# Second MoE of a fused kernel: transfers in multiples of 16 rows, an expert order with 384-place ranks computed rows-first, a last slot in halves, weight loads issued behind the token lists

## The chip, the cores and the metric

One core of a Trainium2 chip runs the whole program. The metric is device time in microseconds (us) of that core, as a median over runs. The engines of a core work side by side, each on its own instruction stream: PE (matmul), DVE (vector), ACT (activations and copies), POOL (GpSimd, which also issues indirect DMAs) and SP (which issues plain DMAs). They wait for each other through semaphores.

## The reference, cut to what matters

Attention with hashed buckets and a first, dense mixture of experts run ahead of the part that changes. What changes is the second mixture: 1536 tokens of width 512, 8 experts of hidden width 1024, each token sent to its two best experts.

```python
def _moe2_ref(x, w_gate, w_noise, noise, w1, w2):
    logits = x @ w_gate
    noise_scale = np.log1p(np.exp(x @ w_noise))
    noisy_logits = logits + noise_scale * noise
    top2 = np.argpartition(-noisy_logits, 2, axis=1)[:, :2]
    ...                                   # softmax over the two: top2_w
    out = np.zeros((N, D), dtype=np.float32)
    for e in range(E):
        for k in range(2):
            mask = top2[:, k] == e
            h = np.maximum(x[mask] @ w1[e], 0.0)
            out[mask] += top2_w[mask, k, None] * (h @ w2[e])
    return out
```

## The kernel before, in words

Every operand of a large matmul is split in two halves of its mantissa (`hh`/`hl` of the hidden values, `w2h`/`w2l` of the weights, `gh`/`gl` of the gathered tokens), and a product is three matmuls: high by high, high by low, low by high.

The router writes, for each token and each of its two experts, a line (token number, weight) into a table in DRAM; an expert's lines lie one behind the other. The experts are then worked off in eight stages, `e` = 0 to 7. Stage 0 is expert 0; half of its 432 places (`EARLY`, 216, two slots of 108) is run ahead, from the tokens that the router knows first, and the other half when all are known. Stages 1 to 7 take the other experts in the order of their token counts: `rank` sorts them, `order` says which expert a stage takes. `CAPS` gives a stage's places, `SLOTS` the number of slots into which they are cut, and `ROWS` the rows of one slot (432 in 4 slots of 108, 384 in 3 of 128, 372 in 3 of 124).

The first layer (`hidden_part`, L238, four parts for a stage) has weights as the stationary side and the tokens as columns: 96 matmuls of as many columns as there are places. The second layer exists in two forms.

- **Turned** (`project_turned`, stages 1 to 6): weights are stationary, 96 matmuls of as many columns as there are places. The result has features on partitions, so it is turned in 32 x 32 blocks (`padded`, `yt`), written to a DRAM scratch `yd` by four stores on SP (`store_turned`, L1271), loaded back with a place on each partition (`ya`, `load_turned`, L1276), scaled on DVE and added to the output by indirect DMAs on POOL (`send`, `scatter`, L1053). The load of stage e is issued on SP when part 0 of stage e+1 is in the queue, and its scaling (`xg<-ya` on DVE) and sends are spread over the second layer of stage e+1; for the last stage they stand at part 2.
- **Rows** (`give`, stages 0 and 7): the hidden values are stationary, and a slot is 24 matmuls of 512 columns whose result has tokens on partitions. It is scaled from PSUM and scattered at once.

The tokens of stage 1 come by one gather a slot (`fetch_rows`, L1226) and 4 transposes on PE for each slot (`turn_rows`, L1030). Those of stages 2 to 7 come in blocks of 32 lines (`fetch_blocks`, L1238: 16 or 12 gathers on POOL, issued two stages ahead) and are turned on DVE (`turn_blocks`). The lists of lines that steer all this (`lts` by rows, `li` and `at` by blocks) are loaded by `list_rows` on SP, each behind a register load of the expert's number.

Weights are fetched on SP into a ring of `stage` tiles (`stage_part`, L173, 512 KB each), split by ACT (high, L180) and DVE (low, L184). The four w2 loads of stage e+1 are issued at the end of stage e: three ahead of the `yd` stores, one behind them.

The change of stage from the first mixture to the second goes so. PE ends the first mixture; `choose` picks experts for the last three tiles of tokens, in two calls with `turn_rows` for the early slots among them. Parts 0 to 2 of the early half of stage 0 follow, with `place` writing the last lines of the table among them. Then w2 of expert 0 is split in two pairs around part 3, the late list `lt` is loaded, two gathers fetch the late slots (L1021), and two early slots run through the second layer in rows. In the second of these, after 18 of its 24 matmuls, stand the transposes of the late slots, which wait for the two gathers. In SP's queue the four w1 loads of stage 1 stand between the first list and the others.

The order of each engine's instructions here is the order of the Python code (`manual_schedule`).

Of the kernel before, what the change touches and what calls it, by code (L numbers as in the profile page):

```python
# [9 lines left out]
F32 = mybir.dt.float32  # L10
F32R = mybir.dt.float32r
BF16 = mybir.dt.bfloat16
I32 = mybir.dt.int32
# [10 lines left out]
CAPS = (432, 432, 416, 400, 400, 384, 384, 372)  # L24
SLOTS = (4, 4, 4, 4, 4, 3, 3, 3)
# [3 lines left out]
ROWS = [c // n for c, n in zip(CAPS, SLOTS)]  # L29
NBLOCK = 4 * SLOT_S  # L30
# [11 lines left out]
def lsh_attention_moe_kernel(ctx, tc, qk, v, proj, probs, w1, w2, w_gate, w_noise, noise, w1b, w2b, out):  # L42
# [45 lines left out]
    caps = const.tile([P, E2], F32, name="caps")  # L88
    for e in range(E2):
        nc.gpsimd.memset(caps[:, e:e + 1], float(CAPS[e]))  # L90
    cum = const.tile([P, E2], F32, name="cum")
# [59 lines left out]
    yd = dram.tile([CAP, DM], F32, name="yd")  # L151
# [112 lines left out]
    def project(o, parts, wt, cols, f0=0, f1=None):  # L264
        for f in range(f0, NF if f1 is None else f1):
            g, ff = divmod(f, 2)
            hh, hl = parts[g]
            wh, wl = wt[g]
            nc.tensor.matmul(o, hh[:, ff, cols], wh[:, ff], start=(f == 0), stop=False)
            nc.tensor.matmul(o, hh[:, ff, cols], wl[:, ff], start=False, stop=False)  # L270
            nc.tensor.matmul(o, hl[:, ff, cols], wh[:, ff], start=False, stop=(f == NF - 1))
# [754 lines left out]
    def turn_rows(rows, s, xgs, n=ROWS[0]):  # L1026
        gh, gl = rows
        pt = small()
        for d in range(ND):
            nc.tensor.transpose(pt[:, d * P:d * P + n], by_chunk(xgs[s], d), ident[:n, :n])  # L1030
# [10 lines left out]

    def put(pool, tag, bufs, ps, lt, s, e):
# [7 lines left out]
    def scatter(y, ps, lt, s, e, view=None):  # L1050
        nc.vector.tensor_scalar_mul(y if view is None else view, ps, lt[:, s, 1:2].bitcast(F32))
        nc.gpsimd.memset(apart, 0.0)
        ins = nc.gpsimd.indirect_dma_start(out=out, out_offset=bass.IndirectOffsetOnAxis(ap=lt[:, s, 0:1], axis=0),  # L1053
# [36 lines left out]
    def rank():  # L1090
# [5 lines left out]
        nc.vector.tensor_tensor(who, key[:, 1:].unsqueeze(1).to_broadcast(sh), iota8[:, 0:K].unsqueeze(2).to_broadcast(sh),  # L1096
# [16 lines left out]
    with tc.manual_schedule(engines={mybir.EngineType.PE}):  # L1113
# [79 lines left out]
    padded = [mp.tile([P, SLOT_S, 4, 32], F32, name=f"padded{i}", bufs=1) for i in range(2)]  # L1193
# [7 lines left out]
    at = mp.tile([P, E2, 4, SLOT_S], I32, name="at", bufs=1)  # L1201
    nc.gpsimd.memset(li, 0)

# [248 lines left out]
```

## Time and profile before

| what | value |
|---|---|
| median of 3 runs | 1089.43 us (1087.86 to 1090.86) |
| profiled execution | 1089.52 us |
| its span, first to last instruction | 1087.8 us |
| mean granted clock of PE | 0.99 |
| PE busy | 1055.6 us, 97% of the span |
| DVE / ACT / POOL busy | 721.2 / 504.9 / 359.0 us |

PE is busy nearly throughout, so what counts are the short stretches in which it stands still or runs at a lower granted clock, the number and width of its matmuls, and what is left to do after its last one. Over the whole span those stretches drown in the means; they are read from the timeline and from windows laid between two first matmuls of neighbouring layers.

### The profile page before, as it was taken

Reading aid. Unit: us, or ns where it says so; the run is one execution under the profiler, and the core shown is the slowest. Engines: PE = TensorE matmul, PEld = TensorE weight load, DVE = VectorE, ACT = ScalarE, POOL = GpSimd, SP = SyncE. Lnnn points to the kernel's source line nnn. Section 1 sums busy time; section 2 is a strip of 40 time slices with the busy share of each in tenths; the row PEclk is TensorE's granted clock in tenths of the full one; section 3 lists DMA queues with packets and bytes.
Section 4 is the critical chain, followed back from the end, with each engine's and each line's share of the span. In section 5 each row is a group of like instructions: output and inputs, shape, how many; then the busy total and the mean of one; then the engine's idle time right before and its main releaser. Section 6 shows DMA issues by size and latency. Waiting matters only on the chain. (4 is left out here: it accounts for less than half of the span.)

```text
span 1087.8 us, 15954 instructions
## 1 busy us (share of the span) xinstructions
PE 1055.6 (97%) x5835; PEld 961.1 (88%) x5836; DVE 721.2 (66%) x1353; ACT 504.9 (46%) x918; POOL 359.0 (33%) x364
## 2 busy tenths in 40 slices
PE   8999999999999999999999999999889999999995
PEld 6999999988888888899888888988778999999993
DVE  7999999978666656647765667545525556765760
ACT  6999999963433333432433342222213334443440
POOL 6587666620000000000000003115336478655533
PEclk9999999999999999999999999999989999999997
DMA  4644444244532112214212225014156468688864
GB/s 134 156 118 117 117 117 118 59 117 135 174 101 78 58 59 78 78 39 136 78 59 59 78 64 164 25 50 79 31 140 183 120 197 219 179 225 222 238 169 56
DMA packets 92781, 125.69 MB, mean 116 GB/s; under 512 B 15882, under 2 KB 59722, under 8 KB 92286
## 3 DMA queue, kind: packets, MB, share of 16 engines
q1 hardware_dynamic: 82522, 110.43, 35.5%
q0 software_dynamic: 9888, 13.92, 6.6%
q8 instruction: 48, 0.79, 0.3%
q14 instruction: 35, 0.29, 0.1%
q10 hardware_dynamic: 288, 0.26, 0.1%
HBM read 92.66 MB, written 20.11 MB: 104 GB/s over the span
## 5 line engine op out<-in xcount | busy, mean ns | idle before, releaser
L182 POOL TENSOR_SCALAR w1h<-stage 128x1024 fp32r<-128x1024 f32 x4 | 5.0, 1257 | 419.4 <-PE sm L723 419.4
L459 DVE TENSOR_TENSOR el<-sm,eh 128x384 fp32r<-128x384 f32 x192 | 102.7, 549 | 17.2 <-ACT eh L458 15.8
L184 DVE TENSOR_TENSOR w2l<-stage,w2h 128x1024 fp32r<-128x1024 f32 x64 | 77.6, 1223 | 49.0 <-ACT w2h L180 35.6
L1238 POOL DMA_INDIRECT xb<-x2d,at x84 | 95.5, 1137 | 25.2 <-issue 24.5
L248 PE MATMUL big<-gh,w1h 128*128 128x216 f32 (+5 forms) x288 | 95.8, 333 | 0.0
L249 PE MATMUL big<-gl,w1h 128*128 128x216 f32 (+5 forms) x288 | 95.1, 330 | 0.0
L250 PE MATMUL big<-gh,w1l 128*128 128x216 f32 (+5 forms) x288 | 95.1, 330 | 0.0
L458 ACT CAST eh<-sm 128x384 fp32r<-128x384 f32 x192 | 86.9, 479 | 16.0 <-PE sm L455 15.4
L728 ACT ACTIVATE hh<-mx 128x384 fp32r<-128x384 f32 x72 | 37.8, 525 | 118.3 <-DVE mx L814 59.6
L403 PE MATMUL big<-k,q 128*128 128x512 f32 (+1 forms) x384 | 90.9, 358 | 1.6 <-POOL k L389 0.7
L455 PE MATMUL sm<-ident,ex 128*128 128x128 f32 x576 | 90.6, 274 | 1.7 <-DVE el L459 1.0
L410 DVE TENSOR_SCALAR_CACHE_REDUCE ms<-big 128x768 f32<-128x768 f32 x96 | 91.0, 948 | 1.8 <-PE big L403 1.5
L422 ACT ACTIVATE ex<-ms,mn 128x768 f32<-128x768 f32 x96 | 90.5, 942 | 3.3 <-DVE ms L410 2.8
L184 DVE TENSOR_TENSOR w1l<-stage,w1h 128x1024 fp32r<-128x1024 f32 x62 | 75.9, 1224 | 19.7 <-ACT w1h L180 16.9
L741 PE MATMUL big<-w2l,hh 128*128 128x512 f32 x224 | 88.4, 395 | 0.0
L742 PE MATMUL big<-w2h,hl 128*128 128x512 f32 x224 | 88.2, 394 | 0.0
L740 PE MATMUL big<-w2h,hh 128*128 128x512 f32 x224 | 88.2, 394 | 0.0
L455 PEld LDWEIGHTS sm<-ident,ex 128*128 128x128 f32 x576 | 70.2, 140 | 12.7 <-DVE el L459 5.6
L253 ACT ACTIVATE hh<-big 128x768 fp32r<-128x768 f32 (+5 forms) x44 | 34.2, 776 | 92.6 <-PE big L250 71.7
L255 DVE SCALAR_TENSOR_TENSOR hl<-big,hh 128x768 fp32r<-128x768 f32 (+5 forms) x44 | 40.1, 910 | 53.9 <-ACT hh L253 49.6
L722 PE MATMUL sm<-xth,w1h 128*128 128x384 f32 x192 | 66.4, 346 | 3.1 <-DVE xa L519 1.2
L1262 PE MATMUL sm<-hl,w2h 128*128 128x400 f32 (+3 forms) x192 | 66.5, 346 | 2.4 <-DVE hl L255 2.4
(289 smaller groups left out, 2929.1 us busy)
## 6 DMA issues: line engine op xcount, KB each, us to landing
stage<-in_moe_w_dram SPq DMA_DIRECT2D x100, 512.0 KB
stage<-in_moe_w_dram SPq DMA_DIRECT2D x58, 256.0 KB
k<-q SPq DMA_DIRECT2D x45, 192.0 KB
z<-in_qk_dram SPq DMA_DIRECT2D x15, 384.0 KB
out_dram<-zero SPq DMA_DIRECT2D x4, 1024.0 KB
vr<-in_v_dram SPq DMA_DIRECT2D x16, 192.0 KB
share<-norms SPq DMA_DIRECT2D x16, 192.0 KB
q<-q SPq DMA_DIRECT2D x15, 192.0 KB
```

Source lines behind the costliest of these rows:

```text
L184: rest.tensor_sub(lo, st, v32(hi))
L248: nc.tensor.matmul(o, wh[:, d, fs], xh[:, d, cols], start=(d == 0), stop=False)
L249: nc.tensor.matmul(o, wh[:, d, fs], xl[:, d, cols], start=False, stop=False)
L250: nc.tensor.matmul(o, wl[:, d, fs], xh[:, d, cols], start=False, stop=(d == ND - 1))
L403: nc.tensor.matmul(ps[:, n0:n1], w_[:, qs], x_[:, n0:n1], start=st, stop=not st)
L410: nc.vector.tensor_scalar(ms, ps[:, :S], MASKED, 3.0e38, op0=ALU.min, op1=ALU.min, accum_out=mn)
L422: nc.scalar.activation(ex, ms, AF.Exp, bias=mn, scale=-1.0, accum_out=recs[u % 2][:, i:i + 1])
L455: nc.tensor.transpose(pt[:, c * P:(c + 1) * P], ex[:, cc * P:(cc + 1) * P], ident)
L459: nc.vector.tensor_sub(el[:, cs, js], ptv, v32(eh)[:, cs, js])
L740: yield lambda: nc.tensor.matmul(outs[j], hh[:, k, js], wh[:, i], start=st, stop=False)
L741: yield lambda: nc.tensor.matmul(outs[j], hh[:, k, js], wl[:, i], start=False, stop=False)
L1238: nc.gpsimd.indirect_dma_start(out=xb[:, b], out_offset=None, in_=x2d.rearrange("t (g x) -> (t g) x", g=4), in_offset=bass.IndirectOffsetO ...
```

## The change

- **Stages and places.** The seven ranks are dealt to the stages by a constant `RANKS`: stage 1 takes the fifth largest expert with 384 places in 3 slots, stages 2 to 5 the four largest (432, 416, 400, 400), stages 6 and 7 the two smallest (384 each, before 384 and 372). Seven more small memsets on POOL in the prologue hold the constant.
- **Second layer by rows.** Where a stage's places are its slots times 128 (`short`: stages 1 and 6, and 7 as before), the second layer runs in rows: `give` for each slot, with no `yd`, `ya` and `send`.
- **Multiples of 16.** In the other stages the loads of `ya` and the sends move `MOVED` rows, which is `ROWS` rounded up to 16 (108, 104 and 100 become 112), and the `yd` stores always move 32 partitions for each block (before 27, 26 or 25). Unused places of `lts` are preset by a memset and an iota on POOL.
- **Last slot in halves.** The last slot of stage 7 runs as two halves of 256 columns, 24 matmuls each; each half is scaled and scattered by itself (rows of 1 KB, `at_half`).
- **Weights behind lists.** The four w1 loads of stage 1 are issued on SP behind all seven lists; the four w2 splits of stage 0 stand ahead of part 3; the second `choose` stands ahead of both `turn_rows`, with 4 filling matmuls (`hum`).

SP, at the change from the first mixture to the second. `lt` is the late list of stage 0, `lts` and `li` the lists of a stage, `stage` the w1 loads of stage 1. Before:

```order
L1016 DMA lt<-table 108x4
L1205 TENSOR_LOAD order
L1205 ISA x2
L1207 ISA
L1207 DMA lts<-table 108x8
L173 ISA
L173 DMA stage<-in_moe_w_dram 128x1024
L173 ISA
L173 DMA stage<-in_moe_w_dram 128x1024
```

and now:

```order
L1021 DMA lt<-table 108x4
L1224 TENSOR_LOAD order
L1224 ISA x2
L1226 ISA
L1226 DMA lts<-table 128x6
L1224 TENSOR_LOAD order
L1224 ISA x2
L1226 ISA
L1226 DMA lts<-table 108x8
L1229 ISA
L1229 DMA li<-table 32x4x8
```

The loads of weights no longer stand behind the first `lts`; the next lists do.

POOL at the same place, where `xg<-x2d,lt` are the late gathers and `xg<-x2d,lts` those of stage 1. Before:

```order
L1195 MEMSET padded_8082 128x512
L1195 MEMSET padded_8083 128x512
L1202 MEMSET li 32x256
L1021 DMA xg<-x2d,lt 108x512 x2
L1226 DMA xg<-x2d,lts 108x512 x4
```

and now:

```order
L1211 MEMSET padded_8092 128x512
L1211 MEMSET padded_8093 128x512
L1219 MEMSET li 32x256
L1220 MEMSET lts 128x64
L1026 DMA xg<-x2d,lt 108x512 x2
L1221 IOTA lts 128x32
L1248 DMA xg<-x2d,lts 128x512 x3
```

A memset of `lts` stands ahead of the late gathers and an iota behind them, which the first `lts` load on SP waits for; stage 1 has three gathers where it had four.

DVE at the end of the program. Before, in stage 7:

```order
L184 TENSOR_TENSOR w2l<-stage,w2h 128x1024
L1051 TENSOR_SCALAR xg<-ya,lts 128x512 x3
L255 SCALAR_TENSOR_TENSOR hl<-big,hh 128x744
L1051 TENSOR_SCALAR xg<-sm,lts 124x512 x3
L1402 TENSOR_LOAD counts
```

and now, in stage 6:

```order
L189 TENSOR_TENSOR w2l<-stage,w2h 128x1024
L1064 TENSOR_SCALAR xg<-ya,lts 112x512 x2
L260 SCALAR_TENSOR_TENSOR hl<-big,hh 128x768
L1064 TENSOR_SCALAR xg<-ya,lts 112x512 x2
L1270 STREAM_TRANSPOSE tb<-xb 128x384
L1274 TENSOR_TENSOR gl<-tb,gh 128x384
```

The scalings of the last turned stage (stage 5) have moved from stage 7 to stage 6; two of them stand ahead of the last `hl` of that stage's first layer.

The diff, cut to its core:

```diff
-CAPS = (432, 432, 416, 400, 400, 384, 384, 372)
-SLOTS = (4, 4, 4, 4, 4, 3, 3, 3)
+CAPS = (432, 384, 432, 416, 400, 400, 384, 384)
+SLOTS = (4, 3, 4, 4, 4, 4, 3, 3)
+RANKS = (4, 0, 1, 2, 3, 5, 6)
 CAP = max(CAPS)
 SLOT_S = max(SLOTS)
 SLOT_P = CAP // SLOT_S
 ROWS = [c // n for c, n in zip(CAPS, SLOTS)]
+MOVED = [-(-r // 16) * 16 for r in ROWS]
...
+    def give_half(y, parts, wt2, lt, s, e, h):
+        ps = small()
+        n = ROWS[e]
+        w = DM // 2
+        hs = slice(h * w, (h + 1) * w)
+        project(ps[:n, :w], parts, wt2, slice(s * n, (s + 1) * n), out=hs)
+        scatter(y[:n, hs], ps[:n, :w], lt[:n], s, e, half=h)
...
-    def scatter(y, ps, lt, s, e, view=None):
+    def scatter(y, ps, lt, s, e, view=None, half=None):
+        rows, o = lt[:, s, 0:1], out
+        if half is not None:
+            rows, o = at_half[:, half:half + 1], out.rearrange("t (h x) -> (t h) x", h=2)
+        ins = nc.gpsimd.indirect_dma_start(out=o, out_offset=bass.IndirectOffsetOnAxis(ap=rows, axis=0),
                                            in_=y, in_offset=None, compute_op=ALU.add)
...
-        nc.vector.tensor_tensor(who, key[:, 1:].unsqueeze(1).to_broadcast(sh), iota8[:, 0:K].unsqueeze(2).to_broadcast(sh),
+        nc.vector.tensor_tensor(who, key[:, 1:].unsqueeze(1).to_broadcast(sh), ranks.unsqueeze(2).to_broadcast(sh),
...
+        chosen.append(choose(tile_logits(turned, 4), t3 + 1, 2))
         first_rows = [ap.tile([P, ND, EARLY], F32R, tag=t, name=t) for t in ("gh", "gl")]
-        turn_rows(first_rows, 0, xgs)
-        chosen.append(choose(tile_logits(turned, 2), t3 + 1, 2))
-        turn_rows(first_rows, 1, xgs)
+        for s in range(early):
+            turn_rows(first_rows, s, xgs)
...
+    at_half = mp.tile([P, 2], I32, name="at_half", bufs=1)
     nc.gpsimd.memset(li, 0)
+    nc.gpsimd.memset(lts, 0)
+    nc.gpsimd.iota(lts[:, :, :, 0], pattern=[[0, E2], [1, SLOT_S]], base=0, channel_multiplier=SLOT_S)
...
-        mine = tv[bass.ds(whose[e], 1), 0:CAPS[e]]
+        mine = tv[bass.ds(whose[e], 1), 0:P * SLOTS[e]]
         nc.sync.dma_start(lts[:ROWS[e], e, :SLOTS[e]].rearrange("p s c -> p (s c)"),
-                          mine.rearrange("o (p s) c -> p (o s c)", s=SLOTS[e]))
+                          mine.rearrange("o (p s) c -> p (o s c)", s=SLOTS[e])[:ROWS[e]])
         if e > 1:
-            nc.sync.dma_start(li[:ROWS[e] // 4, e, :, :SLOTS[e]].rearrange("r b s c -> r b (s c)"),
+            nc.sync.dma_start(li[:, e, :, :SLOTS[e]].rearrange("r b s c -> r b (s c)"),
                               mine.rearrange("o (b r s) c -> r (o b) (s c)", b=4, s=SLOTS[e]))
 
     def list_pieces():
+        for h in range(2):
+            nc.vector.tensor_scalar(at_half[:, h:h + 1], lts[:, E2 - 1, SLOTS[-1] - 1, 0:1], 2.0, float(h),
+                                    op0=ALU.mult, op1=ALU.add)
...
-            xg = slot_tile()[:ROWS[e]]
+            xg = slot_tile()[:MOVED[e]]
             nc.gpsimd.indirect_dma_start(out=xg, out_offset=None, in_=x2d,
-                                         in_offset=bass.IndirectOffsetOnAxis(ap=lts[:ROWS[e], e, s, 0:1], axis=0))
+                                         in_offset=bass.IndirectOffsetOnAxis(ap=lts[:MOVED[e], e, s, 0:1], axis=0))
...
-                            yp[:, :n].rearrange("p s b r -> p (s b) r"))
-
-    def store_turned(yt, e):
+        nc.scalar.copy(yp[:, :, :ROWS[e]], ps[:, :c].rearrange("p (s r) -> p s r", s=n))
+        nc.vector.transpose(yt.rearrange("p s b (k c) -> p k (s b) c", k=ND)[:, d], yp.rearrange("p s (b r) -> p (s b) r", b=4))
+
+    def store_turned(yt):
         for g in range(4):
-            nc.sync.dma_start(yd[0:CAPS[e]].rearrange("(b r s) (g x) -> g r s b x", b=4, s=SLOTS[e], g=4)[g],
-                              yt[32 * g:32 * g + ROWS[e] // 4, :SLOTS[e]])
+            nc.sync.dma_start(yd.rearrange("(b r s) (g x) -> g r s b x", b=4, s=SLOT_S, g=4)[g], yt[32 * g:32 * g + 32])
 
     def load_turned(e):
-        ya = mp.tile([P, SLOT_S, DM], F32, tag="ya", name="ya", bufs=1)[:ROWS[e], :SLOTS[e]]
-        nc.sync.dma_start(ya, yd[0:CAPS[e]].rearrange("(p s) d -> p s d", s=SLOTS[e]))
+        ya = mp.tile([P, SLOT_S, DM], F32, tag="ya", name="ya", bufs=1)
+        nc.sync.dma_start(ya[:MOVED[e]], yd.rearrange("(p s) d -> p s d", s=SLOT_S)[:MOVED[e]])
         return ya
 
 
     def send(s, ya, e):
-        y = slot_tile()[:ROWS[e]]
-        scatter(y, ya[:, s].rearrange("p (g k c) -> p k g c", g=4, k=ND), lts[:ROWS[e], e], s, e,
+        n = MOVED[e]
+        y = slot_tile()[:n]
+        scatter(y, ya[:n, s].rearrange("p (g k c) -> p k g c", g=4, k=ND), lts[:n, e], s, e,
                 y.rearrange("p (k g c) -> p k g c", g=4, k=ND))
+
+    def with_rows(ya, e):
+        return [(s, ya, e) for s in range(SLOTS[e])]
+
+    def short(e):
+        return 0 < e and SLOTS[e] * P == CAPS[e]
 
         wt1 = wt1_next
-        wt2 = [load_w2_part(w2b, 0, r, engine=nc.scalar, staged=staged[r]) for r in (0, 1)]
+        wt2 = [load_w2_part(w2b, 0, r, engine=nc.scalar, staged=staged[r]) for r in range(NP)]
         parts.append(hidden_part(NP - 1, wt1, *first_rows, EARLY, slice(0, EARLY)))
-        wt2 += [load_w2_part(w2b, 0, r, engine=nc.scalar, staged=staged[r]) for r in (2, 3)]
         lt_late, xgs = fetch(mp, SLOT_S, 0, EARLY, early)
         list_rows(1)
-        staged = [stage_part(w1_part(w1b, 1, r), [P, ND, FC]) for r in range(NP)]
         next_xgs = fetch_rows(1)
         for e in range(2, E2):
             list_rows(e)
+        staged = [stage_part(w1_part(w1b, 1, r), [P, ND, FC]) for r in range(NP)]
...
-                if g == 0 and e > 1:
-                    late = [load_turned(e - 1), e - 1]
-                if g == 2 and e == E2 - 1:
-                    for s in range(SLOTS[e - 1]):
-                        send(s, *late)
+                if g == 0:
+                    late = [] if e < 2 or short(e - 1) else with_rows(load_turned(e - 1), e - 1)
+                if g > 1 and short(e):
+                    for _ in range(2 if late else 0):
+                        send(*late.pop(0))
...
+            elif e == E2 - 1:
+                for s in range(SLOTS[e] - 1):
+                    give(mp, "xg", SLOT_S, parts, wt2, lts[:, e], s, e)
+                y = slot_tile()
+                for h in range(2):
+                    give_half(y, parts, wt2, lts[:, e], SLOTS[e] - 1, e, h)
+            elif short(e):
+                prepare(0)
+                for s in range(SLOTS[e]):
+                    prepare(s + 1)
+                    give(mp, "xg", SLOT_S, parts, wt2, lts[:, e], s, e)
+                    fetch_some(s, SLOTS[e])
+                    for r in range(NP * s // SLOTS[e], NP * (s + 1) // SLOTS[e]):
+                        wt1.append(load_w1_part(w1b, e + 1, r, nc.scalar))
             else:
-                for s in range(SLOTS[e]):
-                    give(mp, "xg", SLOT_S, parts, wt2, lts[:, e], s, e)
+                yt = mp.tile([P, SLOT_S, 4, P], F32, tag="yt", name="yt", bufs=1)
+                prepare(0)
+                for d in range(ND):
+                    prepare(d + 1)
+                    project_turned(yt, d, parts, wt2, e)
+                    fetch_some(d, ND)
+                    if late and d > 0:
+                        send(*late.pop(0))
+                    wt1.append(load_w1_part(w1b, e + 1, d, nc.scalar))
+            while late:
+                send(*late.pop(0))
             if 0 < e < E2 - 1:
-                if late:
-                    for s in range(ND - 1, SLOTS[e - 1]):
-                        send(s, *late)
                 ahead = [stage_part(w2_part(w2b, e + 1, r), [P, 2, DM]) for r in range(NP - 1)]
-                store_turned(yt, e)
+                if not short(e):
+                    store_turned(yt)
                 ahead.append(stage_part(w2_part(w2b, e + 1, NP - 1), [P, 2, DM]))
     mp_scope.close()
```

## Rows read from the trace of the kernel before

**Rows 1.** Timeline, PE, at the change to the second mixture (start, us, engine, line, operation, [idle before, releaser])

```profile
763.44 0.73 PE L1030 MATMUL sm<-ident,xg 108*128 108x108 f32 x4 [1.43 <-DMA xg<-x2d,lt]
...
783.73 0.48 PE L269 MATMUL sm<-w2h,hh 128*108 128x512 f32 x1 [0.56 <-ACT w2h L180]
...
784.99 0.49 PE L270 MATMUL sm<-w2l,hh 128*108 128x512 f32 x1 [0.78 <-DVE w2l L184]
...
795.59 0.70 PE L1030 MATMUL sm<-ident,xg 108*128 108x108 f32 x4 [3.70 <-issue]
...
797.83 1.00 PE L1030 MATMUL sm<-ident,xg 108*128 108x108 f32 x4 [1.54 <-DMA xg<-x2d,lt]
...
798.51 0.74 PE L269 MATMUL sm<-w2h,hh 128*108 128x512 f32 x1
```

**Rows 2.** Timeline, POOL: an early gather, and the second of the late ones

```profile
759.66 1.03 POOL L1021 DMA_INDIRECT xg<-x2d,lt  x1 [8.60 <-issue]
...
788.87 1.01 POOL L1021 DMA_INDIRECT xg<-x2d,lt  x1 [0.30 <-issue]
```

**Rows 3.** Timeline, SP's DMA queue: w1 loads of stage 1, the last list

```profile
786.93 2.05 SPq L173 DMA_DIRECT2D stage<-in_moe_w_dram  x4
...
801.53 0.32 SPq L1210 DMA_DIRECT2D li<-table  x1
```

**Rows 4.** Windows, PE (window: us, PE busy (instructions), granted clock, DMA share, GB/s)

```profile
798.51:812.93 14.42, 14.42 (x104) 0.83 0.38 63
844.90:864.33 19.43, 18.99 (x98) 1.00 0.34 108
918.08:935.58 17.50, 17.50 (x98) 1.00 0.77 216
953.14:972.01 18.87, 17.90 (x97) 1.00 0.81 227
988.86:1007.51 18.65, 17.35 (x98) 1.00 0.84 235
1024.31:1041.12 16.81, 16.81 (x98) 1.00 0.81 231
1041.12:1057.49 16.37, 16.37 (x98) 1.00 0.74 193
1057.49:1074.40 16.91, 16.90 (x73) 1.00 0.47 57
```

**Rows 5.** Timeline, DVE and POOL: the last scaling, and two scatters

```profile
1074.43 0.75 DVE L1051 TENSOR_SCALAR xg<-sm,lts 124x512 f32<-124x512 f32 x1 [4.84 <-PE sm L271]
...
1061.21 1.56 POOL L1053 DMA_INDIRECT out_dram<-xg,lts  x1 [0.27 <-issue]
...
1075.49 2.21 POOL L1053 DMA_INDIRECT out_dram<-xg,lts  x1 [3.07 <-DVE xg L1051]
```

**Rows 6.** Windows, POOL, around scatters (window: us, POOL busy, granted clock, DMA share, GB/s)

```profile
1059.50:1066.00 6.50, 3.04 (x4) 1.00 0.99 122
1080.00:1085.00 5.00, 0.00 (x0) 0.50 0.30 47
1085.50:1087.80 2.30, 0.00 (x0) 0.50 0.00 0
```

**Rows 7.** Timeline, ACT and SP's queue: the w2 split, stores and `ya` load, stage 4

```profile
954.61 1.05 ACT L180 CAST w2h<-stage 128x1024 fp32r<-128x1024 f32 x1 [4.83 <-DMA stage<-in_moe_w_dram]
...
939.97 6.35 SPq L1271 DMA_DIRECT2D yd<-yt  x4
...
953.06 0.32 SPq L1276 DMA_DIRECT2D ya<-yd  x1
```

**Rows 8.** Timeline, POOL: a scatter of stage 0, two block gathers

```profile
820.66 1.61 POOL L1053 DMA_INDIRECT out_dram<-y,lt  x1 [16.50 <-DVE y L1051]
...
844.95 0.95 POOL L1238 DMA_INDIRECT xb<-x2d,at  x1 [0.30 <-issue]
...
940.45 1.90 POOL L1238 DMA_INDIRECT xb<-x2d,at  x1 [0.30 <-issue]
```

More of the change, by code (lines that the diff above doesn't have):

```diff
@@ L88, in lsh_attention_moe_kernel @@
     caps = const.tile([P, E2], F32, name="caps")
+    ranks = const.tile([P, E2 - 1], F32, name="ranks")
     for e in range(E2):
         nc.gpsimd.memset(caps[:, e:e + 1], float(CAPS[e]))
+        if e > 0:
+            nc.gpsimd.memset(ranks[:, e - 1:e], float(RANKS[e - 1]))
     cum = const.tile([P, E2], F32, name="cum")
@@ L268, in project @@
             wh, wl = wt[g]
[L269 to L271 removed]
+            nc.tensor.matmul(o, hh[:, ff, cols], wh[:, ff, out], start=(f == 0), stop=False)
+            nc.tensor.matmul(o, hh[:, ff, cols], wl[:, ff, out], start=False, stop=False)
+            nc.tensor.matmul(o, hl[:, ff, cols], wh[:, ff, out], start=False, stop=(f == NF - 1))
     hb = wb = None
@@ L1192, in lsh_attention_moe_kernel @@
     apart = mp.tile([1, 8], F32, name="apart", bufs=1)
-    padded = [mp.tile([P, SLOT_S, 4, 32], F32, name=f"padded{i}", bufs=1) for i in range(2)]
+    padded = [mp.tile([P, SLOT_S, P], F32, name=f"padded{i}", bufs=1) for i in range(2)]
     for t in padded:
@@ L1336, in lsh_attention_moe_kernel, with prepare, fetch_some @@
                 rows = new_rows(CAPS[e + 1])
-            if 0 < e < E2 - 1:
-                yt = mp.tile([P, SLOT_S, 4, P], F32, tag="yt", name="yt", bufs=1)
-                if e + 2 < E2:
-                    xbs[e + 2] = blocks()
-                turn_blocks(rows, 0, e + 1)
-                for d in range(ND):
-                    if d + 1 < ND:
-                        turn_blocks(rows, d + 1, e + 1)
-                    project_turned(yt, d, parts, wt2, e)
-                    if e == 1:
-                        follow(rows[1][:, d])
-                        fetch_blocks(3, 2 * d, 2 * d + 2)
-                    elif e + 2 < E2:
-                        each = SLOTS[e + 2]
-                        fetch_blocks(e + 2, each * d, each * d + each)
-                    if late and 0 < d <= SLOTS[e - 1]:
-                        send(d - 1, *late)
-                    wt1.append(load_w1_part(w1b, e + 1, d, nc.scalar))
-            elif e == 0:
+            if 0 < e < E2 - 1 and e + 2 < E2:
+                xbs[e + 2] = blocks()
+            def prepare(d):
+                if d < ND:
+                    turn_blocks(rows, d, e + 1)
+            def fetch_some(d, n):
+                if e == 1:
+                    follow(rows[1][:, d])
+                    fetch_blocks(3, 8 * d // n, 8 * (d + 1) // n)
+                elif e + 2 < E2:
+                    each = 4 * SLOTS[e + 2]
+                    fetch_blocks(e + 2, each * d // n, each * (d + 1) // n)
+            if e == 0:
                 for s in range(early):
-                    for r in range(s * SLOTS[1] // early, (s + 1) * SLOTS[1] // early):
+                    each = [SLOTS[1] * (s + x) // early for x in (0, 1)]
+                    for r in range(*each):
                         turn_rows(rows, r, next_xgs, ROWS[1])
+                    for r in range(NP * s // early, NP * (s + 1) // early):
                         wt1.append(load_w1_part(w1b, e + 1, r, nc.scalar, staged[r]))
```

18 lines of the change are left out of this document (7 added, 11 removed).

## The prediction

> **What bounds the kernel now.** PE is busy for 97% of the span, so the sum has to come from three things: stretches in which PE stands still or runs at a lower granted clock, the width and number of its matmuls, and what is left after its last one. I read them in this order. First PE's timeline where the first mixture hands over to the second [rows 1]: PE waits 1.43 us for an early gather, 0.56 and 0.78 us for the w2 splits, and then 3.70 and 1.54 us in the middle of a second layer, for the two late gathers. POOL has issued the second of these at 788.87 [rows 2]; PE's transposes of it begin at 797.83, 8.96 us later. For the early gather the same way took 763.44 - 759.66 = 3.78 us. What stands beside the slow one and not beside the fast one are four w1 loads of 512 KB, issued on SP from 786.93 on [rows 3]. Second, windows from one layer's first matmul to the next [rows 4]: the stretch behind the late gathers has a granted clock of 0.83, and two second layers of one width differ (400 columns: 17.50 and 18.87 us; 384 columns: 16.81 and 18.65). Third the tail: PE's last layer ends at 1074.40 [rows 4], the span at 1087.8, 13.4 us later.
>
> **A, the hand-over: -7.1 us.** The second `choose` now stands ahead of the transposes that wait 1.43 us, so its matmuls fill that wait. I take 1.0 of the 1.43 as won, and the chain to the late list and gathers as 1.0 earlier: the second late gather at 787.87 on POOL. The w1 loads leave SP's queue at this point; what stands there now are lists of some KB each, and the loads come behind the last list, at about 801 [rows 3]. If the gather then lands as the early one did, PE has it at 787.87 + 3.78 = 791.65, and after the four transposes (798.51 - 797.83 = 0.68) its matmuls go on at 792.33 instead of 798.51: -6.2. The two w2 waits (1.34 together) lie inside that wait and give nothing more while the gathers end last. Of the clock: 798.51 to 812.93 took 14.42 us at 0.83; at full clock 0.83 x 14.42 = 12.0 to 12.4 would do, so some 2.0 are lost there. PE still pauses for the gathers, only for less long, so I give back 0.5. Stage 1 has three slots instead of four: four transposes fewer, of which a group takes 0.70 [rows 1] and overlaps its neighbours in part: -0.45. Bounds: the gathers were held by something else and only the 1.0 and the 0.45 come, -1.5; all of the gather's excess, the clock and the early wait come, -(6.2 + 0.4 + 2.0 + 0.45 + 1.34) = -10.4. I take the value by the uncontended gather, since it is the same instruction with the same bytes 29 us earlier.
>
> New in POOL's queue there: a memset of `lts` ahead of the late gathers, which falls into the time in which POOL waits for the list, and an iota behind them, for which the first `lts` load on SP waits. Behind that load in SP's queue stand all other lists and the w1 loads. First need of the w1 loads is stage 1's first layer, which PE reaches some 25 us after the late gathers; lists of about 12 us and loads of about 10 us have room there. I cost it at nothing; if not covered, it is the few us by which the lists start later.
>
> **B, PE's work: +0.6 us.** The seven ranks have the same widths in another order, but the last has 384 places instead of 372: its first layer 16.81 instead of 16.37 (16.81 is the same number of matmuls with 384 columns), +0.44 [rows 4]. A second layer by rows is 72 matmuls of 512 columns, 16.91 us, and turned 96 of 384, 16.81: two more stages by rows, +0.2. The halves are 48 matmuls of 256 columns for 24 of 512: at half of 16.91 / 72 = 235 ns they are free, and that I take. The nearest row below 512 is 384 columns at 16.81 / 96 = 175 ns; at that, 48 x (175 - 117) = +2.8. Bounds +0.6 to +3.4.
>
> **C, the stalls in the second layers: -1.65 us.** Stage 1's window holds 19.43 - 18.99 = 0.44 of idle time; stage 4's is 18.87 - 17.50 = 1.37 over its twin, stage 5's 18.65 - 16.81 = 1.84 [rows 4]: 3.65 in all. In stage 4 ACT waits 4.83 us for a w2 tile [rows 7], whose load stands on SP behind the four `yd` stores (6.35 us of issuing). These move 25 partitions each; 32 partitions should spread over more DMA engines, as the 128-row scatters do against the 124-row one [rows 6]. Stage 2 now follows a stage without `yd`, stage 7 too. Against it: more bytes per store, and in stage 6 two scalings of `ya` stand on DVE ahead of the last `hl` of the first layer. `ya` was issued 953.06 - 935.58 = 17.5 us into its stage [rows 4, 7]; with stores that end earlier I estimate 13 (issuing ended 939.97 + 6.35 - 935.58 = 10.7 into the stage, and 2.2 to land as a 128-row scatter does [rows 6]), and the last `hl` is needed about 16.8 + 18/24 of a slot's 5.6 (24 x 235 ns) = 21 us in. So it fits by some us, or, if `ya` stays at 17.5 and takes 6.5 us (near the late gather's 8.96), PE waits 3. I take 2.0 of stalls left, -1.65; bounds -3.65 to +3.
>
> **D, the tail: -6.3 us.** Before: PE's end to POOL's start 1075.49 - 1074.40 = 1.09, of which the DVE scaling is 0.75; POOL's 2.21; then data until at most 1085.5 at a DMA share of 0.30, nearly five of 16 engines; then 2.3 us with none [rows 5, 6]. The three 128-row scatters ahead of it moved at a share of 0.99 and took 6.5 / 3 = 2.2 us each; POOL needs 1.56 for one. After: 128 rows of 1 KB in the last piece. Scaling half as wide, 0.83 to POOL's start; 1.56 on POOL; data 2.4 (half of 2.2, and 1.3 to begin: the last of the three ended 1066.0 - (1061.21 + 1.56) = 3.2 behind POOL, less 2.2, rounded up); 2.3 at the end: 7.1 instead of 13.4. Bounds: nothing by the halves (the rival below) and a slower start, -4.7; no start-up, -7.4.
>
> The Trainium skill has a rule that speaks against the halves ("DMA: Bandwidth & Descriptors", section "Anatomy of one DMA — SWDGE (gpsimd) path"): a DMA issued by GpSimd takes about 2.0 us fixed plus its bytes over 436 GB/s. By it, as an estimate from that page, a half saves 0.3 us over a whole slot (2.3 for 2.6). The trace doesn't agree for 124 rows, which took until about 8 us after POOL's end [rows 5, 6]. The same page (section "Why a DMA increments its semaphore by 16 and not by 1") says that the row count sets the number of DMA engines, the largest divisor up to 16, so 4 for 124 rows and 16 for 128 or 112; shares of 0.30 and 0.99 agree roughly, and for 112 rows no run here shows it.
>
> **Sum.** -7.1 + 0.6 - 1.65 - 6.3 = -14.5, against the profiled execution's 1089.52 (0.1 above the median): **1075.0 us**.
>
> **The rivals.**
> - *The late gathers are held by something other than the w1 loads* (the table's scatters, or POOL's descriptors): A is -1.5 instead of -7.1, 1080.6. For it: PE's 3.70 is named as no semaphore's. Against: the DMA queue and the gather of 3.78. Chance 0.13. With C at its bad end as well it comes to about 1085, within 0.3%.
> - *Halves give nothing*, because a scatter costs by its packets and not by its bytes (128 packets either way, 2.2 us whole or half), and the second half waits behind the first: scaling 0.83, data 2.2 + 1.5: 1076.5. [...] Chance 0.14.
> - *The multiples of 16 don't spread*: what is fast at 128 rows isn't so at 112, and the 32-partition stores only add bytes: C is +3 instead of -1.65, 1079.7. No 112-row transfer is in the trace. Chance 0.07.
> - *`ya` blocks DVE in stage 6* (above): +3, 1078. Chance 0.06.
> - *Slower: POOL's block gathers become the bound in stages 1 and 2.* Two stages' gathers (32) now run beside three more scatters in stage 1. A gather costs 0.95 + 0.30 where none stands beside it and 1.90 + 0.30 beside scatters and `yd` [rows 8]. If all 32 go at the slow price, 32 x 0.95 = 30 us, PE waits in stages 2 and 3 for its tokens: 1105. It decides from where the excess passes the gain of 14.5: 14.5 / 32 = 0.45 us per gather, a mean of 1.7 us. Against: stage 1's scatters come one per 5.6 us of PE, and gathers stand two stages ahead of their use. Chance 0.05.
>
> **How the numbers follow.** The forecast has the rest, 0.55, at 1075.0. The range reaches on the low side to 1069 (A and C near their good ends: -3.3 and -2), on the high side to 1083 (A's and C's bad ends singly, or the halves at 175 ns with one of the rivals); the slower case and the doubled one stay out, and some of the low end. About 0.3%, 3.3 us, is what a measurement tells from no change: all cases but the last are faster, less the part of the first that ends within it. Faster 0.89, the same 0.06, slower 0.05.
>
> **What would show it.** A: PE's waits for the late transposes fall from 3.70 and 1.54 to about 2 together, four w1 loads behind the last list, granted clock over 798 to 813 nearer 1. If the loads are gone from there and the wait is still 5 us, A is wrong. B: second layers by rows at 16.9, 48 matmuls of the halves in 5.6 us; 8 would be the upper bound. C: second layers of stages 4 and 5 within 0.5 of 17.5, ACT's wait for w2 under 4 us; a DVE wait for `ya` ahead of the last `hl` of stage 6 would be the fourth rival. D: PE's end to the span's end near 7 us, and a DMA share near 0.9 in the last data stretch. Gathers on POOL with PE waiting for `xb`'s transposes at stages 2 and 3 would be the slower case.

## The result, and the profile after

| | before | after |
|---|---|---|
| median | 1089.23 us (4 runs, 1087.86 to 1090.86) | 1071.51 us (4 runs, 1070.29 to 1072.63) |
| ratio, 95% interval | | 0.9836 (0.9819 to 0.9854) |
| span of the profiled execution | 1087.8 us | 1070.9 us |
| mean granted clock of PE | 0.99 | 0.997 |

The forecast was 1075.0, range 1069 to 1083. A second set of runs gave the same (1072.91 us). In a third, on another chip than the second, the same kernel took 1097.34 us against 1090.94 before, 1.0064 (1.0046 to 1.0082); the experiments on the gathers below are about that.

Windows of the changed kernel on PE, against [rows 4] (window: us, PE busy (instructions), granted clock, DMA share, GB/s; the granted clock is a mean over the window, 1.00 being the upper level of 2.4 GHz and 0.50 the lower of 1.2): rest of stage 0's early part and late first layer, second layers of stages 1, 4, 5 and 6, all of stage 7's second layer.

```profile
792.77:806.66 13.89, 13.89 (x109) 0.90 0.73 159
835.50:852.12 16.62, 16.62 (x74) 1.00 0.36 97
943.37:960.87 17.50, 17.50 (x98) 1.00 0.70 219
978.31:995.81 17.50, 17.50 (x98) 1.00 0.77 229
1012.54:1030.00 17.46, 16.91 (x74) 1.00 0.93 228
1046.74:1063.70 16.96, 16.96 (x97) 1.00 0.25 33
```

Stages 4 and 5 now take 17.50 each where [rows 4] have 18.87 for stage 4; only stage 6 has idle time, 0.55. The timeline at the late gathers (start, us, engine, line, operation, [idle before, releaser]), against [rows 1, 2]:

```profile
788.44 1.01 POOL L1026 DMA_INDIRECT xg<-x2d,lt  x1 [0.30 <-issue]
...
790.83 0.70 PE L1035 MATMUL sm<-ident,xg 108*128 108x108 f32 x4 [0.96 <-issue]
...
792.09 0.99 PE L1035 MATMUL sm<-ident,xg 108*128 108x108 f32 x4 [0.56 <-DMA xg<-x2d,lt]
```

From POOL's issue to the transposes the second late gather takes 3.65 us; it was 8.96. PE waits 0.96 + 0.56 where it waited 3.70 + 1.54. Stage 6 (SP's queue, DVE, PE) and the end of the program (DVE, POOL, two windows on POOL):

```profile
1007.12 0.34 SPq L1296 DMA_DIRECT2D ya<-yd  x1
...
1016.08 0.88 DVE L1064 TENSOR_SCALAR xg<-ya,lts 112x512 f32<-112x512 f32 x2 [3.44 <-DMA ya<-yd]
...
1017.88 0.50 PE L276 MATMUL sm<-w2h,hl 128*128 128x512 f32 x1 [0.55 <-DVE hl L260]
...
1063.74 0.48 DVE L1064 TENSOR_SCALAR xg<-sm,lts 128x256 f32<-128x256 f32 x1 [2.37 <-PE sm L276]
...
1064.50 1.56 POOL L1069 DMA_INDIRECT out_dram<-xg,at_half  x1 [1.26 <-DVE xg L1064]
...
1066.00:1068.20 2.20, 0.07 (x1) 1.00 0.58 67
1068.60:1070.90 2.30, 0.00 (x0) 0.51 0.00 0
```

`ya` is issued 1007.12 - 995.81 = 11.3 us into stage 6, and DVE still waits for it ahead of the last `hl`. PE ends at 1063.70, the span 7.2 us later.

Where the 16.9 us between the two spans went: stage 1 begins at 818.76 instead of 825.93 (-7.2, although PE ran 1.3 us behind when the first mixture ended); stages 1 to 7 take 244.9 instead of 248.5 (-3.5); the tail 7.2 instead of 13.4 (-6.2).

### The profile page after: what moved, and what is told of

The parts are those of the page before. It is cut to its first block, busy times and chain, and to the rows that moved or that the text cites. A ratio compares the mean times of both kernels' runs of the same rounds, so it can differ in the third digit from the quotient of the medians.

```text
span 1070.9 us, 15896 instructions
## 1 busy us (share of the span) xinstructions
PE 1053.9 (98%) x5809; PEld 955.6 (89%) x5810; DVE 720.8 (67%) x1347; ACT 502.6 (47%) x909; POOL 354.4 (33%) x377
## 5 line engine op out<-in xcount | busy, mean ns | idle before, releaser
L254 PE MATMUL big<-gl,w1h 128*128 128x384 f32 (+4 forms) x288 | 94.5, 328 | 0.3 <-DVE gl L1039 0.3
L253 PE MATMUL big<-gh,w1h 128*128 128x384 f32 (+4 forms) x288 | 94.9, 329 | 0.0
L255 PE MATMUL big<-gh,w1l 128*128 128x384 f32 (+4 forms) x288 | 94.5, 328 | 0.0
L189 DVE TENSOR_TENSOR w1l<-stage,w1h 128x1024 fp32r<-128x1024 f32 x62 | 75.4, 1221 | 12.6 <-ACT w1h L185 9.9
L260 DVE SCALAR_TENSOR_TENSOR hl<-big,hh 128x768 fp32r<-128x768 f32 (+4 forms) x44 | 40.2, 914 | 60.1 <-ACT hh L258 60.0
L258 ACT ACTIVATE hh<-big 128x768 fp32r<-128x768 f32 (+4 forms) x44 | 34.2, 778 | 96.7 <-PE big L255 90.9
L734 DVE SCALAR_TENSOR_TENSOR hl<-mx,hh 128x384 fp32r<-128x384 f32 x72 | 41.0, 570 | 41.4 <-ACT hh L733 41.4
```

The lines of the kernel that those rows point to most:

```text
L189: rest.tensor_sub(lo, st, v32(hi))
L253: nc.tensor.matmul(o, wh[:, d, fs], xh[:, d, cols], start=(d == 0), stop=False)
L254: nc.tensor.matmul(o, wh[:, d, fs], xl[:, d, cols], start=False, stop=False)
L255: nc.tensor.matmul(o, wl[:, d, fs], xh[:, d, cols], start=False, stop=(d == ND - 1))
```

## The experiments

Times are medians with the kernel before run beside them on the same chip. Six of the variants of the changed kernel show a slow stretch in stage 2 that the run of the result does not have; they are read from their windows and timelines, and the stretch comes last.

**The hand-over: the loads.** One part alone, in the kernel before:

```diff
-        staged = [stage_part(w1_part(w1b, 1, r), [P, ND, FC]) for r in range(NP)]
         next_xgs = fetch_rows(1)
         for e in range(2, E2):
             list_rows(e)
+        staged = [stage_part(w1_part(w1b, 1, r), [P, ND, FC]) for r in range(NP)]
```

> The kernel before with one part of the change alone: the four w1 loads of stage 1 behind all seven lists. Theory: the second late gather reaches PE 3.7 us after its issue instead of 9.0, PE's waits of 3.70 and 1.54 us shrink to less than 1.5 together, and the whole is about 5 us shorter, 1084. Rival (other parts of the change freed the gathers): 1089.

1084.68 us against 1090.92, 0.9940 (0.9920 to 0.9961). The timeline, POOL and PE:

```profile
791.46 1.01 POOL L1021 DMA_INDIRECT xg<-x2d,lt  x1 [0.30 <-issue]
...
794.46 1.30 PE L1030 MATMUL sm<-ident,xg 108*128 108x108 f32 x8
```

3.0 us from issue to transposes, and no wait. From the early second layer's first matmul to its restart behind the late transposes it is 12.6 us; in the kernel before it is 18.3. This one move carries the term: 6.2 us of the whole, 4.3 to 8.7 by the interval.

The opposite, in the changed kernel (the `staged` line back between `list_rows(1)` and `fetch_rows(1)`):

> The changed kernel with one part undone: the four w1 loads of stage 1 stand again behind the first list on SP, ahead of the second layer of stage 0. Theory (the late gathers were held by these loads): PE's waits for the two late gathers go from 0.96 and 0.56 us to about 5 together, the way from POOL's issue of the second late gather to its transposes from 3.65 to about 9 us, and the whole is 5 to 6 us longer than the changed kernel, about 1077. In this kernel the first list also waits for POOL's iota, behind the late gathers, so the loads start some 3 us later than they did before; if the loads then miss the gathers, the waits stay near 1.5 us and so does the time. Rival (the gathers were freed by the earlier choice of experts, or by the other order on POOL): no change, 1071.5, whenever the loads run.

```profile
789.95 1.93 SPq L178 DMA_DIRECT2D stage<-in_moe_w_dram  x4
...
790.53 0.70 PE L1035 MATMUL sm<-ident,xg 108*128 108x108 f32 x4 [0.63 <-issue]
791.83 0.73 PE L1035 MATMUL sm<-ident,xg 108*128 108x108 f32 x4 [0.59 <-DMA xg<-x2d,lt]
```

PE's waits are 0.63 and 0.59 us, together no longer than in the changed kernel, though the loads stand in their old place in the queue: SP issues them from 789.95 on, where before it was 786.93. The first list now waits for POOL's iota behind the late gathers, and both gathers have landed by 791.83, 1.9 us behind the first load's issue. By itself this run also fits its rival; together with the first one it says that the overlap in time is what cost, and that in the changed kernel the iota is enough to end it. The iota alone in the kernel before wasn't tried. The whole (1097.52) is that of the stretch in stage 2.

**The hand-over: the choice of experts.** The second `choose` back between the two `turn_rows`, without `hum`:

> The changed kernel with the second choice of experts again between the two transposes of early rows, without the filling matmuls. Theory: PE waits about 1.4 us for the early gather, and everything up to the late gathers comes 1 to 1.5 us later, since the chain to these (table, list, gather) starts at that choice; +1.3 us. Rival: the late gathers' own wait of 1.5 us takes it up, 0. Read from the start of stage 0's first layer and of stage 1, and not from the whole, if the stretch in stage 2 appears.

The wait for the early gather is 0.54 us, but stage 1 begins at 820.41, and at 816.83 in the changed kernel on the same chip. The expected 1.3 us became 3.6. Most of it goes with the clock: from 764 to 776 the granted clock is 0.72 here, so PE ran part of that time at the lower level,

```profile
764.00:776.00 12.00, 11.53 (x73) 0.72 0.15 40
```

and 1.00 in the changed kernel on the same chip. The two kernels differ in the order, in the four filling matmuls and by half a microsecond of idle time; which of these holds the clock wasn't tried apart. The whole is 1073.70 and 1072.91, which can't be told apart; in the profiled executions 1.9 of the 3.6 us are left at the end (stage 6 has no wait here, its `ya` landing 19.0 us into the stage instead of 20.5).

**The yd stores: partitions or order?** Each of the four stores in two, 25 and 7 partitions, or 16 and 16 (the control):

```diff
-            nc.sync.dma_start(yd.rearrange(...)[g], yt[32 * g:32 * g + 32])
+            for r0, r1 in ((0, 25), (25, 32)):
+                nc.sync.dma_start(yd.rearrange(...)[g, r0:r1], yt[32 * g + r0:32 * g + r1])
```

> The changed kernel with each of the four yd stores of a stage cut in two by partitions, 25 and 7 of 32. Theory (the stalls of the kernel before came from stores of 27, 26 or 25 partitions, which move on few DMA engines, and the w2 load and ya behind them): the second layers of stages 4 and 5 grow from 17.5 us to 18.5 or more, ya in stage 6 is issued 3 to 6 us later than 11.3 us into its stage, and the whole is 2 to 4 us longer than the changed kernel. Rival (the other order of stages took the stalls away): second layers stay at 17.5, and so does the time.

> The control to the one with 25 and 7: also eight stores a stage instead of four, but 16 and 16 partitions. Theory: the issuing of four more stores costs SP some us, but second layers stay at 17.5 us and the time within 1 us of the changed kernel. Rival (the number of stores counts, not their partitions): like 25 and 7.

Windows of the second layers of stages 4, 5 and 6, first 25 and 7:

```profile
971.11:995.77 24.66, 20.71 (x98) 0.86 0.73 214
1013.21:1037.32 24.11, 20.22 (x97) 0.86 0.73 223
1054.06:1079.52 25.46, 19.50 (x73) 0.87 0.83 223
```

then 16 and 16:

```profile
969.66:987.16 17.50, 17.50 (x98) 1.00 0.82 253
1004.60:1022.63 18.03, 17.76 (x97) 1.00 0.83 246
1039.37:1060.70 21.33, 18.48 (x74) 0.92 0.92 229
```

Same bytes, same number of stores, same chip: 1117.32 and 1104.20 us, 13 us where the theory had 2 to 4. It is the partition count. The way it works is the one of [rows 7], ACT's wait for the last w2 tile of a stage, whose load stands behind the stores: in the kernel before 4.83 us in stage 4 and 5.03 in stage 5, in the changed kernel none in either (first line: stage 4) and 0.96 in stage 6, with 25 and 7 partitions 7.10, 8.09 and 7.62 in stages 4 to 6 (second line: stage 6), with 16 and 16 0.65, 3.10 and 2.89. With 25 and 7, PE then waits 3.2 us twice for ACT's `hh`.

```profile
939.94 1.04 ACT L185 CAST w2h<-stage 128x1024 fp32r<-128x1024 f32 x1
```

```profile
1058.50 1.04 ACT L185 CAST w2h<-stage 128x1024 fp32r<-128x1024 f32 x1 [7.62 <-DMA stage<-in_moe_w_dram]
```

The control isn't free, as its theory had it: in stage 6 it loses 4 us. Eight stores take 8.39 us of issuing there instead of 5.12, its `ya` lands 22.6 us into the stage, and PE waits 2.85. No run has the old counts (27, 26 and 25 partitions) in four stores of the changed kernel, so how much of the gain is theirs, and how much the other order of stages gives, isn't measured.

The ya loads and sends at their exact rows (`MOVED = list(ROWS)`), stores as changed:

> The changed kernel with the ya loads and the sends of stages 2 to 5 at their exact rows (108, 104, 100) instead of 112; the stores keep 32 partitions. Theory: these transfers run on fewer DMA engines and land later, but beside PE's work and ahead of need; ya in stage 6 lands 1 to 2 us later, so that PE's wait for the last hl there grows from 0.55 to about 1.5, and the whole by about 1 us. Rival (the 112 rows carry the gain of the stores' neighbours too, for instance through POOL's scatters and block gathers): second layers over 17.5 us, 2 us or more.

Second layers of stages 4 and 5 are 17.50 and 17.49; stage 6 is 21.43, with a PE wait of 2.97 and `ya` landing 22.7 us into the stage, where the changed kernel has it at 20.3:

```profile
1034.56 0.31 SPq L1296 DMA_DIRECT2D ya<-yd  x1
...
1043.33 0.88 DVE L1064 TENSOR_SCALAR xg<-ya,lts 100x512 f32<-100x512 f32 x2 [4.79 <-DMA ya<-yd]
```

The theory has the wrong step. From issue to landing the load takes 8.8 us with 100 rows and 9.0 with 112 in the run of the result, so the load itself is no slower. It is issued later, 13.9 us into the stage instead of 11.3, behind the `yd` stores and the w2 load that follows them. Other executions with 112 rows and four stores issue it 10.6 to 12.6 us into the stage, so 1.3 us or more go with the exact rows, by one execution; whether through the loads or the sends of the stage ahead wasn't tried apart. The stage stands so near its limit that twice the expected wait came of it.

**Rows in stages 1 and 6, or turned** (`short(e)` true for stage 7 alone):

> The changed kernel with the turned second layer in stages 1 and 6 as well (384 places, 96 matmuls of 384 columns), the sends of stage 6 in stage 7's parts 2 and 3. Theory: PE's own work is the same (16.8 for 16.7 us), and what the form by rows takes away are yd stores, the ya load and its waits: here 0 to 2 us longer, by stalls in stages 2 and 7 and none in stage 6. Rival (rows are what freed the second layers): stalls of 1 to 2 us again in stages 4 and 5.

Stages 4 and 5 are 17.49, stage 6 16.81 with no wait: the form by rows did not free them. 1077.79 us, on a chip where three other variants were over 1100, since its stage 2 has almost none of the stretch below; the expected 0 to 2 us can't be read from that, as the changed kernel wasn't run on this chip.

**The tail.** The last slot whole (`give` for all three slots); and with 372 places, 124 rows, the halves kept:

> The changed kernel with the last slot whole: 24 matmuls of 512 columns, one scaling of 128 x 512 and one scatter of 128 rows of 2 KB. Theory by bytes: the last scaling is 0.27 us longer (0.75 for 0.48) and the last data 1.1 us longer, PE's work 0.2 shorter (5.87 to 5.64), so PE's end to the span's end goes from 7.2 to 8.6 and the whole is 1.2 longer, 1072.7. Rival by packets (128 either way): only the scaling is longer, tail 7.5, and with PE's 0.2 the time is that of the changed kernel, 1071.5.

> The changed kernel with 372 places in the last stage again, so that its slots have 124 rows; the halves stay. Theory (the row count, and not the halves, makes the tail): the DMA share in the last data stretch falls from about 0.6 to 0.3, a half of 124 rows takes 3 to 4 us longer to land than one of 128, the tail is 10 to 11.5 us instead of 7.2, PE's work 0.4 shorter in the first layer, and the whole 3 to 4 us longer, about 1075. Rival (the halves make the tail): tail about 7.5, time 1071.4.

From PE's end to the span's end it is 7.8 us with a whole slot of 128 rows (1097.4 - 1089.60, one execution). With halves of 128 rows nine executions of the changed kernel and its variants give 6.8 to 8.4, 7.7 in the mean (the variant with turned stages, whose sends stand in POOL's way there, has 9.8). With halves of 124 rows it is 9.9, with a whole slot of 124 it was 13.4. The windows of the last data, 128 whole and 124 in halves:

```profile
1092.80:1095.00 2.20, 0.00 (x0) 0.77 0.87 118
```

```profile
1091.10:1095.50 4.40, 0.01 (x1) 0.63 0.55 73
```

At 128 rows the halves save nothing that shows beside that spread (the rival by packets), at 124 they save 3.5 us. The row count made the term.

**The stretch in stage 2.** The changed kernel itself, twice more on other chips:

> The changed kernel itself, unaltered. Three variants of it, two of which differ from it only behind stage 6, show a stretch of 25 us in the second layer of stage 2 in which PE's matmuls start 0.7, 1.4 or 2.1 us apart with no wait named, beside POOL's block gathers, and end 26 us later. First reading: the stretch hangs on a small difference of these variants (what stands in memory where, or times that differ by 0.1 us), and the changed kernel runs at 1071.5 as it did. Second reading: it hangs on the chip or the moment, and the changed kernel shows it as well, about 1097, while the kernel before stays near 1090.

> The changed kernel unaltered once more, beside the one with the gathers spread on the same chip. If the stretch in stage 2 hangs on the chip, this one has it where its variants had it (about 1097) or not at all (1071 to 1073); six variants with the same order on PE, POOL and DVE up to stage 2 had it on two chips, this kernel and one variant had it not on two others.

The first: 1072.91 against 1086.34, 0.9862 (0.9815 to 0.9909). The second: 1097.34 against 1090.94. Its second layer of stage 2 takes 41.30 us, 18.77 on the other chip:

```profile
869.95:911.25 41.30, 25.63 (x97) 0.71 0.27 85
```

POOL and PE around it:

```profile
873.61 0.97 POOL L1260 DMA_INDIRECT xb<-x2d,at  x1 [0.16 <-issue]
...
886.15 0.35 PE L1284 MATMUL sm<-hl,w2h 128*128 128x432 f32 x1 [1.05 <-issue]
888.24 0.52 PE L1285 MATMUL sm<-hh,w2l 128*128 128x432 f32 x1 [1.74 <-issue]
...
906.09 0.94 POOL L1260 DMA_INDIRECT xb<-x2d,at  x1 [0.30 <-issue]
...
909.34 0.72 PE L1283 MATMUL sm<-hh,w2h 128*128 128x432 f32 x1 [0.19 <-issue]
```

PE waits for no semaphore that the trace names ("issue"), and its matmuls start about 0.7, 1.4, 2.1 or 2.8 us apart instead of 0.2. Beside it POOL issues block gathers one behind the other, most of them every 1.25 us with 0.3 us between, from 873.61 without a break to 907.0. In all seven executions that have the stretch it starts 10.4 to 11.1 us behind the beginning of this string of 26 gathers and ends 2.3 to 3.1 us behind its last one. (The string begins 3.65 us behind the start of stage 2's second layer in each of them, so these seven alone could also mean a place in PE's program.) In the kernel before, the scaled sends of stage 1, which wait for DVE, cut the string in groups, of ten at most; stage 1 by rows has no sends left for stage 2. With stage 1 turned the string begins 1.0 us ahead of that layer and is ten gathers long, 872.47 to 884.68, and PE is slow from 883.5 to 887 only: again 11 us behind the beginning, and 2.3 behind the end. But ten in a row needn't do it: the version with the loads alone moved has ten from 877.95 to 890.26, on a chip where three variants show the stretch, and no slow PE.

So the gathers were spread, and two edits added for the waits seen above, which stand ahead of stage 2 and behind it:

```diff
+                elif e == 2:
+                    follow(yt[:, 0, 0, 32 * d:])       # wait for this quarter's result
+                    fetch_blocks(4, 2 * d, 2 * d + 2)
...
+                if e == 3:
+                    follow(parts[g][1][:, 0])
+                    fetch_blocks(4, 8 + 2 * g, 10 + 2 * g)
...
-                if g > 1 and short(e):
-                    for _ in range(2 if late else 0):
+                if g == NP - 1 and short(e):
+                    for _ in range(len(late)):
...
-            turn_rows(rows, s, xgs)
+            turn_rows(rows, s, xgs, spare=(4, 2)[s])   # filling matmuls ahead
```

> The changed kernel with three edits: the 16 block gathers of stage 4's tokens, which stand in one string behind those of stage 3's in POOL's queue, are cut into pairs (four behind the quarters of stage 2's second layer, four behind the parts of stage 3's first layer), so that no string is longer than a few gathers; six filling matmuls stand in PE's waits for the two late gathers; and the four sends in stage 6 stand behind its last hl. Theory (some 20 us of unbroken gathers on POOL are what slows PE's issue in stage 2 where it is slowed, until 3 us behind the last of them): the second layer of stage 2 takes 18.8 us on every chip, and the whole is about 1071 or less (0.5 to 3 us by stage 6, 1 to 1.4 us by the clock behind the late gathers). Rival (the place in PE's program, or the chip alone): where the changed kernel has the 22 us stretch in stage 2, this one has it too.

1077.32 against 1090.94 on the chip where the changed kernel took 1097.34: 0.9875 (0.9858 to 0.9892). Second layer of stage 2, first layer of stage 4, second layer of stage 6:

```profile
873.70:892.46 18.76, 18.76 (x97) 1.00 0.27 82
928.88:950.78 21.90, 19.55 (x97) 0.92 0.84 221
1019.95:1036.57 16.62, 16.62 (x73) 1.00 0.95 232
```

The stretch is gone, at the same place of PE's program and on the same chip. 1071 was missed: 4.5 us went in stage 4, whose tokens now come late, and stage 1 begins 2.7 us later than in the changed kernel beside it (820.60 for 817.88), where PE waits 1.88 us for an `hl` of stage 0 that DVE wrote late, which is left unexplained; the sends behind the last `hl` take stage 6 to 16.62 (17.07 in the changed kernel beside it). The filling matmuls gave little: PE is back at 792.11 instead of 792.52, and the clock right behind is at its upper level in both. On that chip this version beats both kernels; where there is no stretch it wasn't run.

## Why the prediction was right, and where not

**A, -7.1; measured -7.2.** The cause stands: the loads held the late gathers, 3.65 us against the 3.78 that the early gather gave. That the sizes agree to 0.1 is luck in part. PE was 1.3 us behind when the first mixture ended. So it is in all twelve profiled executions of the changed kernel and its variants (761.0 to 761.5 us, against 760.0 and 759.7 with the kernel before and its one variant): a cost of the change that the sum puts at nothing, and whose cause is open. Against it, the earlier choice gave more than the 1.0 taken: from there to stage 0's first layer it is 6.9 us instead of 8.6. But it was put in the wrong place: the wait it fills (0.54 in the experiment) is worth less than the granted clock that goes with it, 0.72 against 1.00 over 12 us. Behind the late transposes 1.4 us came (the clock, and four transposes fewer) where 0.95 was taken. Nothing was lost by the later w1 loads, as costed.

**B, +0.6; measured -0.4** (stages 1 to 7 are 3.5 us shorter, and C has 3.1 of that). The last rank cost 0.37 (16.74 for 16.37). By rows, stage 1's second layer took 16.62, 0.2 less than the 16.81 turned; stage 6's is 16.91 busy with a wait inside, and 16.62 in the version without that wait; +0.1 each was taken. The halves took 5.87 us for 48 matmuls, 122 ns each where 117 were taken. What the sum doesn't have is that layers of the same width ran shorter (432 columns: 18.71 and 18.76 us for 18.97 and 18.99 busy), which is left unexplained.

**C, -1.65; measured -3.1.** Mis-sized: 3.65 of stalls became 0.55, not 2.0. The mechanism was right by the control: stores of 25 and 7 partitions give second layers of 24.7 us where 16 and 16 give 17.5, through ACT's wait for w2. That fits the Trainium skill's rule in "DMA: Bandwidth & Descriptors" (section "Why a DMA increments its semaphore by 16 and not by 1"), by which the partition count's largest divisor up to 16 sets the number of DMA engines, 5 and 7 against 16; no row here counts the engines. What is left is the fourth rival's place, `ya` ahead of the last `hl` of stage 6, 0.2 to 0.7 us in the changed kernel and not 3. There two steps of the estimate were off against each other: `ya` was issued at 11.3 us and not 13, and took 9.0 to land where the bad case has 6.5. The margin was as thin as feared, 3 us of wait where `ya` landed 2.4 later.

**D, -6.3; measured -6.2.** Right in size by a wrong step. "Half of 2.2" for the data of a half was by bytes; the whole slot ends within the spread of the halves. The rival "halves give nothing" was the true one as far as that spread shows, at 7.8 us of tail instead of the 8.4 that its terms add up to (0.83 + 1.56 + 2.2 + 1.5 + 2.3). The term is 124 to 128 rows. The DMA share near 0.9 that was to show it is 0.58 with halves and 0.87 with the whole slot.

One reading in the rivals is wrong: 1085 is 4.3 us from 1089.5, 0.4%, and so not "within 0.3%"; it touches only the chance of "the same".

**The slower rival.** It was given 0.05, with POOL's gathers of stages 1 and 2 as its place and 30 us as its price. In the third set of runs it decided the sign, with 22.5 us (41.30 less 18.77) in just that place. So the forecast holds for the chips of the result and of the second set, and it is luck that the result was taken where there is no stretch. The rival's mechanism was wrong: PE doesn't wait for tokens. What matters instead is that the sends of stage 1, which broke up the string in stage 2, are gone: with them back, or with the gathers spread, the stretch shrinks to 3.5 us or is gone. The order of POOL shows the string ahead of any run: 2, 16 and 8 gathers for stages 3 to 5, back to back behind the last `follow`. Why the runs of the result and the second set have the same string and no stretch is not explained (the chip, or the moment), and nor is what in PE's path to its next instruction is held up.

## What to carry to other kernels

Give a DMA on the path a partition or row count that is a multiple of 16 before cutting it in pieces: the count was worth 5.6 us at the tail (13.4 to 7.8), and with it right the pieces gave nothing that showed. When a gather is late, look at what else moves in the same microseconds; an iota that made the loads start 3 us later did as much here as another order. A change that takes work out of an engine's queue also takes out its pauses: look at what stands back to back afterwards, and run it on more than one chip.

## What the runs showed of the hardware

- **Long strings of indirect gathers slow PE's issue, but not everywhere.** Some 11 us of gathers issued with 0.3 us between them, then matmuls 0.7 to 2.8 us apart until 2.3 to 3.1 us behind the last gather: seven executions on three chips. The same string of 26 (874.48 to 910.67) left PE alone in the run of the result, and so it did on a fourth chip; ten in a row left it alone on two of the three (877.95 to 890.26 with the loads alone moved, 913.72 to 926.1 with the gathers spread) and slowed it for 3.5 us on the other. What is held up between POOL and PE is open.
- **The partition count of a store can cost more than its bytes.** Splitting 32 partitions 25 and 7 made three second layers 17 us longer together than 16 and 16, with the same bytes.
- **The row count of a scatter sets how soon it lands.** Behind POOL's end the last data of 124 rows of 2 KB took 7.8 us, and of 128 rows of 2 KB 2.8 us.
- **The granted clock can cost more than the wait ahead of it:** a wait of 0.54 us, in another order and without four filling matmuls, went with 0.72 instead of 1.00 over 12 us, about 3 us. No rule comes out of these runs: behind waits of 1.0 and 0.6 us at the late gathers, with no filling, the clock was 0.90 in the run of the result (792.77 to 806.66) and 1.00 on another chip (793.97 to 805.50).
